# A state-space layer mixed with a feed-forward layer: own states for even tokens, B without scaling, and the skip as diagonal products

## Chip, core and metric

The kernel runs on one core of a Trainium2 chip. The metric is device time in microseconds (us) of one execution. Ratios are the mean time of one kernel's fast runs over the mean of the other's fast runs of the same rounds, so they are not quite the ratio of the medians that are quoted beside them. The profile's *span* runs from the first to the last instruction; the time is 1.7 to 2.1 us longer than the span.

Engines: PE (TensorE, matrix products), PEld (its weight loads, which overlap PE), DVE (VectorE), ACT (ScalarE), POOL (GpSimd), SP (SyncE, which issues most DMAs). PE's matmuls are pipelined: the mean length of one is not its cost, the distance to the next start is (448 columns: 0.35 us mean length, 0.19 us from start to start).

## The reference, cut to what matters

```python
# x: [1, 2048, 448] bf16; B, C: complex 448 x 448; Lambda, Dskip: 448; w1: 448 x 1792; w2: 1792 x 448
g = sigmoid((x * gate_w).sum(-1))
Lam_bar = exp(exp(log_dt) * Lam);  B_bar = ((Lam_bar - 1) / Lam)[:, None] * B
h[t] = Lam_bar * h[t-1] + B_bar @ x[t]                   # complex, 2048 steps
a = 2 * real(h @ C.T) + x * Dskip
b = silu(x @ w1) @ w2
out = g * a + (1 - g) * b
```

Both kernels take tokens in pairs: row k holds tokens 2k (even) and 2k+1 (odd). The 448 complex states lie in seven tiles of 128 rows: three pairs (real, imaginary) and one tile with 64 real and 64 imaginary rows. The recurrence over 1024 pairs is a scan on VectorE, turned into a real one by cos/sin tables.

## The kernel before

It builds `Lambda*B` on VectorE, so one product gives the input of a whole pair, and it scans only the odd tokens' states. The even token's output comes from the odd state before it, through a second matrix `CE` (C times Lambda), and from its own x through a dense matrix `K0 = C B + diag(Dskip)`:

```python
def bu(m, h):                       # input of a pair of tokens: 7 products of full height
    for j in range(7):
        pe.matmul(ps[bank], LT[:, m, j, :], XT[:, j, h*512:(h+1)*512], start=(j == 0), stop=(j == 6))
# ... (cut)
def k0(j):                          # K0, block j of 4
    for m in range(7):
        pe.matmul(ps[0:M, bank, 0:D], BB[:, m, D+j*128:D+j*128+M], CO[:, m, :], ...)
    pe.matmul(ps[0:M, bank, j*128:j*128+M], ID[:, 0:M], DE[:, j, 0:M], ...)        # + diag(Dskip)
# ... (cut)
def ytile(kt, odd):                 # output of 128 tokens
    for m in range(7):
        pe.matmul(ps[:, bank, 0:D], HS[:, m, o0:o0+128], C[:, m, :], ...)          # C = CO if odd else CE
    if not odd:
        for j in range(4):
            pe.matmul(ps[:, bank, 0:D], XT[:, j, t0:t0+128], KT[:, j, :], ...)     # x @ K0
    # DVE: out = gate * ps + BG (odd; BG = gate*x*Dskip + b, two DVE operations) or + b (even)
# ... (cut) the order near the end of PE's program
ffn2(3, 0); ffn2(3, 1)
for j in range(4): k0(j)
ffn2(3, 2); ffn2(3, 3)
for q in range(4): ytile(q, 0); ytile(q, 1); skip(q + 4); store(q)
for kt in range(4, 8): ytile(kt, 0); ytile(kt, 1); store(kt)
```

Of the kernel before, what the change touches and what calls it, by code (L numbers as in the profile page):

```python
# [146 lines left out]
def gated_mix(nc, A_x, A_Lambda_re, A_Lambda_im, A_B_re, A_B_im, A_C_re, A_C_im, A_log_dt,  # L147
              A_Dskip, B_x, B_w1, B_w2, gate_w, out):
    with ExitStack() as ctx:
# [9 lines left out]
        XT = sb("XT", [128, 7, NK], BF16)  # L159
        W1E = sb("W1E", [128, 4, F_FF], BF16)  # L160
        W1O = sb("W1O", [128, 4, F_FF], BF16)
        W2 = sb("W2", [128, NFB, D], BF16)
        BB = sb("BB", [128, 7, 2 * D], BF16)
        Y3 = sb("Y3", [128, 2, D], BF16)
        LT = sb("LT", [128, 8, 7, 128], BF16)
# [3 lines left out]
        CE = sb("CE", [128, 8, D], BF16)  # L169
        KT = sb("KT", [128, 4, D], BF16)  # L170
        DE = sb("DE", [128, 4, 128], BF16)
        DBC = sb("DBC", [128, D], BF16)
# [3 lines left out]
        HS = sb("HS", [128, 8, NK + 8], BF16)  # L176
        AT = [sb(f"AT{i}", [128, NFB, 512], BF16) for i in range(2)]
        OT = [sb(f"OT{i}", [128, 2 * D], BF16) for i in range(3)]
        GWB = sb("GWB", [128, D], BF16)
        JK = sb("JK", [128, 2, D], BF16)  # L180
# [4 lines left out]
        TMPS = [sb(f"TMP{i}", [128, D], F32) for i in range(2)]  # L185
# [9 lines left out]
        W1EF = W1E[:, :, :].rearrange("p a b -> p (a b)")  # L195
        XO = W1EF[:, 0:NKT * D].rearrange("p (k c) -> p k c", k=NKT)
        BG = W1EF[:, NKT * D:].bitcast(F32).rearrange("p (k c) -> p k c", k=4)
        LTF = LT[:, :, :, :].rearrange("p a b c -> p (a b c)")

        def bs(tile):  # L200
            return LTF[:, tile * D:(tile + 1) * D]

# [7 lines left out]
        def ldt(dst, src, key, reads=(), group=None):  # L210
            return T.dma("sp", lambda e: e.dma_start_transpose(dst, src), reads=reads,
                         writes=[key], group=group)

        XE = [[f"XTe0{j}" for j in range(4)], ["XTe1"] * 4]

        def swap_xr(eng, h):
            hs = slice(h * 512, (h + 1) * 512)
            T.op(eng, lambda e: e.tensor_copy(XR[64:128, hs], XT[0:64, 3, hs]), reads=XE[h][3:],
                 writes=[f"XR{h}a"])
            T.op(eng, lambda e: e.tensor_copy(XR[0:64, hs], XT[64:128, 3, hs]), reads=XE[h][3:],  # L220
                 writes=[f"XR{h}b"])
# [28 lines left out]
        T.op("act", lambda e: e.activation(JK[:, 0, 0:1], HP[:, :], AF.Exp), reads=["HP"], writes=["JK0"])  # L250
        ld("act", W1E[64:128, 3, :], B_w1[384:448, :], "W1Ez")
        ld("sp", BB[:, 0:6:2, D:], A_B_re[0:384, :].rearrange("(t p) d -> p t d", p=128), "Bre", gB)
        ld("sp", BB[:, 1:6:2, D:], A_B_im[0:384, :].rearrange("(t p) d -> p t d", p=128), "Bim", gB)
        ldt(XT[:, 0:4, 512:1024], x2[512:1024, 0:512], "XTe1")
        gB3 = T.group()
        for i, src in enumerate((A_B_re, A_B_im)):
            for h in range(2):
                ld("sp", Y3[h * 64:(h + 1) * 64, i, :], src[384:448, :], f"By{i}{h}", gB3)
        for h in range(2):
            ldt(XT[:, 4:7, h * 512:(h + 1) * 512], x2[h * 512:(h + 1) * 512, 512:896], f"XTo{h}")  # L260
        B_RAW = ["Bre", "Bim"]
        XC_ALL = ["XC0", "XC1"] + [f"XC3_{q}" for q in range(4)]
        B3 = ["By00", "By01", "By10", "By11"]

# [8 lines left out]
        T.op("pool", lambda e: e.memset(KT[64:128, 3, :], 0.0), writes=["KTz"])  # L273
        swap_xr("pool", 1)
# [10 lines left out]
        def ffn1_mm(c, fbs):  # L285
# [3 lines left out]
            W, w0, x0, jr = (W1O, 1, 4, 0) if odd else (W1E, 0, 0, 3)  # L289
            banks = [nxt() for _ in fbs]  # L290
            xk = XE[h] + [f"XTo{h}"] if odd else XE[h]

            for fb, bank in zip(fbs, banks):
                def mm(pe, fb=fb, bank=bank):
                    ins = None
                    for j in range(3):
                        ins = pe.matmul(ps[:, bank, :], W[:, w0 + j, fb * 128:(fb + 1) * 128],  # L297
                                        XT[:, x0 + j, hs], start=(j == 0), stop=False)
                    return ins
                wk = ["W1Ob"] if odd else ["W1Ej0", "W1Ej1", "W1Ej2"] if fb < NFA else ["W1Ed"]  # L300
                T.op("pe", mm, reads=wk + xk, writes=[f"ps{bank}"])

            def rest(pe):
                ins = None
                for i, (fb, bank) in enumerate(zip(fbs, banks)):
                    up = (i % 2 == 1) != bool(odd)
                    p = slice(64, 128) if up else slice(0, 64)
                    x = XT[p, 3, hs] if up == bool(odd) else XR[p, hs]
                    ins = pe.matmul(ps[:, bank, :], W[p, jr, fb * 128:(fb + 1) * 128], x,  # L309
                                    start=False, stop=True)  # L310
                return ins
            wk = ["W1Oa", "W1Oz"] if odd else ["W1Ea", "W1Ez"]
            T.op("pe", rest, reads=wk + xk + [f"XR{h}a", f"XR{h}b"],
                 writes=[f"ps{bank}" for bank in banks])
# [18 lines left out]
        def ffn1_act(c, fb, bank):  # L333
            a = AT[c % 2]
            T.op("act", lambda e: e.activation(a[:, fb, :], ps[:, bank, :], AF.Silu),  # L335
                 reads=[f"ps{bank}"], writes=[f"AT{c % 2}_{fb}"])

        def ffn1(c, f0=0):
            for f in range(f0, NFB, 4):
                for fb, bank in ffn1_mm(c, list(range(f, min(f + 4, NFB)))):  # L340
                    ffn1_act(c, fb, bank)
                    yield fb
# [32 lines left out]
        T.op("dve", lambda e: e.tensor_copy(XR[0:64, 0:512], xp[3][64:128, :]), reads=["ps6"], writes=["XR0b"])  # L375
# [36 lines left out]
        pact("dt", LDT, AF.Exp, ["PV"])  # L412
        ptt("ar", col("dt"), LRE, ALU.mult, ["dt", "PV"])
        pact("mag", col("ar"), AF.Exp, ["ar"])
        T.op("act", lambda e: e.activation(JK[:, 0, 0:1], HP[:, :], AF.Silu), reads=["HP"], writes=["JK0"])
        ptt("ph", col("dt"), LIM, ALU.mult, ["dt", "PV"])
# [3 lines left out]
        pts("nfr", col("fr"), -1.0, None, ALU.mult, ALU.bypass, ["fr"])  # L420
        ptt("afr", col("fr"), col("nfr"), ALU.max, ["fr", "nfr"])
        pact("sn", col("fr"), AF.Sin, ["fr"], scale=SIN_SCALE)
        pact("cs", col("afr"), AF.Sin, ["afr", "HP"], scale=-SIN_SCALE, bias=HP[:, 0:1])
        ptt("t0", LRE, LRE, ALU.mult, ["PV"])
        ptt("t1", LIM, LIM, ALU.mult, ["PV"])
        ptt("t0", col("t0"), col("t1"), ALU.add, ["t0", "t1"])
        T.op("dve", lambda e: e.reciprocal(col("rden"), col("t0")), reads=["t0"], writes=["rden"])
        ptt("lr", col("mag"), col("cs"), ALU.mult, ["mag", "cs"])
        ptt("li", col("mag"), col("sn"), ALU.mult, ["mag", "sn"])
        pts("nli", col("li"), -1.0, None, ALU.mult, ALU.bypass, ["li"])  # L430
        for o, up, low in (("ba", "lr", "li"), ("bb", "nli", "lr")):
            for a, b, n in ((0, 64, up), (64, 128, low)):
                T.op("dve", lambda e, o=o, a=a, b=b, n=n: e.tensor_copy(
                    P[a:b, pc(o), 3:4], P[a:b, pc(n), 3:4]), reads=[n], writes=[o])
        pc("dr")

# [5 lines left out]
            reads=["f2"] + SGN, writes=["f2s"])  # L442
        ptt("rr", col("mag"), col("mag"), ALU.mult, ["mag"])


        def phase(pt):
            return HS[:, 2 * pt:2 * pt + 2, :].rearrange("p a b -> p (a b)")[:, 0:2 * NK].bitcast(F32)

        def phases(pt):
            f2 = "f2s" if pt == 3 else "f2"  # L450
            X, RR = phase(pt), G[:, 1, :]
            T.op("dve", lambda e: e.tensor_scalar(X, IOTA[:, :], c1(f2, pt), None, ALU.mult),
                 reads=["IOTA", f2], writes=[f"F{pt}"])
            T.op("dve", lambda e: e.tensor_scalar(RR, X, MAGIC, -MAGIC, ALU.add, ALU.add),
                 reads=[f"F{pt}"], writes=["G1"])
            T.op("dve", lambda e: e.tensor_tensor(X, X, RR, ALU.subtract),
                 reads=[f"F{pt}", "G1"], writes=[f"F{pt}"])

        def tables(pt):
            X = phase(pt)  # L460
            T.op("act", lambda e: e.activation(SIN[:, pt, :], X, AF.Sin, scale=SIN_SCALE),
# [7 lines left out]
            T.op("pool", lambda e: e.memset(HS[:, 2 * pt:2 * pt + 2, 0:8], 0.0),  # L469
                 writes=[f"F{pt}", f"HSz{pt}"])  # L470
# [3 lines left out]
        n_tmp = [0]  # L474

        def lincombs(items):

            ts = []
            for dst, key, x, xs, y, ys, reads in items:
                t = n_tmp[0] % 2  # L480
                n_tmp[0] += 1
                ts.append(t)
                T.op("dve", lambda e, t=t, y=y, ys=ys: e.tensor_scalar(TMPS[t][:, :], y, ys, None, ALU.mult),
                     reads=reads, writes=[f"TMP{t}"])
            for (dst, key, x, xs, y, ys, reads), t in zip(items, ts):
                T.op("dve", lambda e, t=t, dst=dst, x=x, xs=xs: e.scalar_tensor_tensor(
                    dst, x, xs, TMPS[t][:, :], ALU.mult, ALU.add),
                    reads=list(reads) + [f"TMP{t}"], writes=[key])

        def step_B(pt):  # L490
            if pt < 3:
                lincombs([(BB[:, m, 0:D], f"BB{m}", BB[:, m, D:], c1("lr", pt), BB[:, m ^ 1, D:],
# [288 lines left out]
        for fb in ffn1(1):  # L781
            if fb % 3 == 1:
                run(tabs, 1)
# [91 lines left out]
```

## Time and profile before

| | |
|---|---|
| time, median of 3 runs | 154.72 us (154.54 to 158.25) |
| span of the profiled execution | 154.1 us |
| PE / DVE / ACT busy | 96% / 78% / 41% |

First the page of the kernel before: busy times of each engine, and its chain of waits by engine. The chain is followed back from the last instruction, at each step to what released it.

```profile
PE 148.0 (96%) x749; PEld 67.6 (44%) x749; DVE 120.2 (78%) x233; ACT 63.8 (41%) x111; POOL 5.5 (4%) x15
...
PE 91%; DMA 5%; SPq 1%; DVE 0%; issue 0%
```

The same chain in order of time (start, length, what):

```profile
2.46 8.44 DMA W1E<-in_B_w_dram
...
10.94 3.30 PE ps L324 x14
14.24 2.70 PE ps L297 x12
...
31.48 21.26 PE ps L643 x98
...
112.66 1.32 PE ps L658 x7
113.98 0.06 PE ps L660
...
123.67 1.32 PE ps L738 x7
125.00 0.76 PE ps L742 x4
125.75 2.65 PE ps L738 x14
...
150.95 0.68 DVE OT L750
```

From 10.94 us on, each piece starts where the last ended: the time is the sum of PE's work. L297 (with the half-height L309) belongs to the first feed-forward product, L627 to the second (FFN2), L658 and L660 are K0, L738 the state products of the output, L742 the even tiles' `x @ K0`, L643 the products by B.

Groups of instructions of the kernel before (line, engine, operation, shapes, count; then busy us, mean ns of one; then idle before):

```profile
L676 DVE TENSOR_TENSOR Q<-G,COS 128x1024 bf16<-128x1024 f32 x7 | 8.5, 1211 | 0.0
L676 DVE TENSOR_TENSOR Q<-HS,COS 128x1024 bf16<-128x1024 bf16 x7 | 4.8, 685 | 0.0
L486 DVE SCALAR_TENSOR_TENSOR CO<-XC,P,TMP 128x448 bf16<-128x448 bf16 x7 | 4.5, 673 | 0.0
```

These are VectorE's prices: 0.69 us for a 1024-wide product of two bf16 tiles, 1.21 us with a float32 input, and 0.67 us for a 448-wide scalar_tensor_tensor. What the prediction below calls "one element a cycle" is about 1.04 ns per element.

### The profile page before, as it was taken

How to read it: one execution, taken by the hardware profiler on the slowest of the kernel's cores; microseconds unless marked ns; L12 is line 12 of the kernel's file. 1: busy time of each engine (PE TensorE's matmuls, PEld its weight loads, DVE VectorE, ACT ScalarE, POOL GpSimd, SP SyncE). 2: the span in 40 equal slices, each digit the busy share in tenths (PEclk: the TensorE clock that was granted, in tenths of full speed). 3: DMA queues.
4: the chain of work that ended last, by engine and by line, in shares of the span. 5: the costliest groups of instructions: out<-in, count | busy, mean ns of one | idle time of the engine just before them, and what ended most of it. 6: DMA issues, size and time to landing. Idle time of an engine off the chain costs nothing.

```text
span 154.1 us, 1999 instructions
## 1 busy us (share of the span) xinstructions
PE 148.0 (96%) x749; PEld 67.6 (44%) x749; DVE 120.2 (78%) x233; ACT 63.8 (41%) x111; POOL 5.5 (4%) x15
## 2 busy tenths in 40 slices
PE   6879999999999999999999999999999999999991
PEld 2323333344444455433455333555555555555550
DVE  1653913999999999999999999999999218885341
ACT  1256748999976600555731166612233110000000
POOL 7000040000000000000000000000000000000000
PEclk9999999999999999999999999999999999999999
DMA  4999999998942930004834500000000001112211
GB/s 125 279 234 226 221 355 164 219 175 147 345 124 55 304 117 0 0 22 93 156 85 96 187 0 4 0 2 0 0 0 4 0 0 60 60 60 83 100 60 60
DMA packets 26225, 16.25 MB, mean 105 GB/s; under 512 B 17892, under 2 KB 25320, under 8 KB 26216
## 3 DMA queue, kind: packets, MB, share of 16 engines
q1 hardware_dynamic: 24452, 13.23, 35.2%
q10 hardware_dynamic: 1764, 2.90, 7.2%
q8 instruction: 6, 0.10, 0.3%
q14 instruction: 3, 0.02, 0.0%
HBM read 9.93 MB, written 1.84 MB: 76 GB/s over the span
## 4 chain that ended last, share of the span: by engine, by line
PE 91%; DMA 5%; SPq 1%; DVE 0%; issue 0%
PE ps L627 28%; PE ps L297 21%; PE ps L643 14%; PE ps L738 14%; DMA W1E<-in_B_w_dram 5%; PE ps L309 4%; PE ps L742 4%; PE ps L658 4%; PE ps L324 2%; SPq L208 1%; DVE OT L750 0%; SPq L237 0%; PE ps L660 0%
## 5 line engine op out<-in xcount | busy, mean ns | idle before, releaser
L627 PE MATMUL ps<-W,AT 128*128 128x448 bf16 x224 | 43.1, 353 | 0.0
L335 ACT ACTIVATE AT<-ps 128x512 bf16<-128x512 f32 x56 | 29.0, 606 | 13.9 <-PE ps L309 11.9
L627 PEld LDWEIGHTS ps<-W,AT 128*128 128x128 bf16 x224 | 21.7, 98 | 20.6 <-ACT AT L335 0.5
L632 ACT ACTIVATE LT<-ps,GT 128x448 bf16<-128x448 f32 x16 | 9.8, 634 | 32.8 <-PE ps L627 23.2
L643 PE MATMUL ps<-XT,LT 128*128 128x512 bf16 x98 | 21.3, 379 | 0.0
L297 PE MATMUL ps<-XT,W1O 128*128 128x512 bf16 x84 | 19.5, 380 | 0.0
L679 DVE TENSOR_TENSOR_SCAN G<-P,Q 128x1024 f32<-128x1024 f32 x7 | 15.7, 2277 | 0.0
L297 PE MATMUL ps<-XT,W1E 128*128 128x512 bf16 x63 | 14.6, 380 | 0.0
L643 PEld LDWEIGHTS ps<-XT,LT 128*128 128x128 bf16 x98 | 9.5, 98 | 11.5 <-issue 0.2
L750 DVE SCALAR_TENSOR_TENSOR OT<-ps,GT,LT 128x448 bf16<-128x448 f32 x8 | 5.5, 684 | 9.7 <-PE ps L742 9.6
L297 PEld LDWEIGHTS ps<-XT,W1O 128*128 128x128 bf16 x84 | 7.7, 98 | 10.9 <-issue 2.5
L738 PE MATMUL ps<-CE,HS 128*128 128x448 bf16 x56 | 11.9, 352 | 0.0
L738 PE MATMUL ps<-CO,HS 128*128 128x448 bf16 x56 | 11.9, 352 | 0.0
L750 DVE SCALAR_TENSOR_TENSOR OT<-ps,GT,W1E 128x448 bf16<-128x448 f32 x8 | 5.5, 684 | 5.1 <-PE ps L738 5.1
L297 PEld LDWEIGHTS ps<-XT,W1E 128*128 128x128 bf16 x63 | 5.7, 98 | 8.6 <-issue 1.7
L647 ACT ACTIVATE HS<-ps 128x512 bf16<-128x512 f32 x14 | 8.0, 609 | 2.6 <-PE ps L643 2.0
L594 DVE SCALAR_TENSOR_TENSOR JK<-W1O,GWB 128x448 bf16<-128x448 bf16 x16 | 8.8, 621 | 0.0
L676 DVE TENSOR_TENSOR Q<-G,SIN 128x1024 bf16<-128x1024 f32 x7 | 8.5, 1220 | 0.0
L676 DVE TENSOR_TENSOR Q<-G,COS 128x1024 bf16<-128x1024 f32 x7 | 8.5, 1211 | 0.0
L324 PE MATMUL ps<-XT,W1E 128*128 128x512 bf16 (+1 forms) x28 | 6.8, 379 | 1.3 <-DMA W1E<-in_B_w_dram 1.0
L738 PEld LDWEIGHTS ps<-CE,HS 128*128 128x128 bf16 x56 | 5.5, 98 | 5.1
L738 PEld LDWEIGHTS ps<-CO,HS 128*128 128x128 bf16 x56 | 5.5, 98 | 5.1
(84 smaller groups left out, 147.5 us busy)
## 6 DMA issues: line engine op xcount, KB each, us to landing
W1O<-in_A_x_dram ACTq DMA_DIRECT2D x1, 1792.0 KB, 11.6
out_dram<-OT SPq DMA_DIRECT2D x8, 224.0 KB, 1.9
W<-in_B_w_dram SPq DMA_DIRECT2D x1, 1568.0 KB, 7.7
W1O<-in_B_w_dram SPq DMA_DIRECT2D x1, 1344.0 KB, 8.4
W1E<-in_A_x_dram SPq DMA_DIRECT2D x1, 896.0 KB, 6.2
W1E<-in_B_w_dram ACTq DMA_DIRECT2D x3, 224.0 KB, 7.4
W1E<-in_B_w_dram SPq DMA_DIRECT2D x1, 672.0 KB, 10.4
W1E<-in_B_w_dram SPq DMA_DIRECT2D x2, 224.0 KB, 6.3
```

Of the source, the lines that this page charges most:

```text
L297: ins = pe.matmul(ps[:, bank, :], W[:, w0 + j, fb * 128:(fb + 1) * 128], XT[:, x0 + j, hs], start=(j == 0), stop=False)
L324: T.op("pe", lambda pe, fb=fb, bank=bank, j=j, p=p: pe.matmul(ps[:, bank, :], W1E[p, j, fb * 128:(fb + 1) * 128], XT[p, j, 0:512], start=( ...
L335: T.op("act", lambda e: e.activation(a[:, fb, :], ps[:, bank, :], AF.Silu), reads=[f"ps{bank}"], writes=[f"AT{c % 2}_{fb}"])
L594: T.op("dve", lambda e, t=t: e.scalar_tensor_tensor(JK[:, t % 2, :], XN[:, t * D:(t + 1) * D], 1.0, GWB[:, :], ALU.mult, ALU.mult, accum_o ...
L627: ins = pe.matmul(ps[:, bank, 0:D], a[:, fb, q * 128:(q + 1) * 128], W2[:, fb, :], start=(fb == 0), stop=(fb == NFB - 1))
L632: T.op("act", lambda e: e.activation(bs(tile), ps[:, bank, 0:D], AF.Copy, scale=GT[:, 2, tile:tile + 1]), reads=[f"ps{bank}", "GT2"], writ ...
L643: ins = pe.matmul(ps[:, bank, :], LT[:, m, j, :], XT[:, j, h * 512:(h + 1) * 512], start=(j == 0), stop=(j == 6))
L647: T.op("act", lambda e: e.activation(HS[:, m, 8 + h * 512:8 + (h + 1) * 512], ps[:, bank, :], AF.Copy), reads=[f"ps{bank}", f"F{pt}"], wri ...
L676: T.op("dve", lambda e: e.tensor_tensor(o, a, b, op), reads=reads, writes=writes)
L679: T.op("dve", lambda e: e.tensor_tensor_scan(G[:, c, :], rb, Q1[:, c, :], 0.0, ALU.mult, ALU.add), reads=[f"Q1{c}", "rr"], writes=[f"G{c}"])
L738: ins = pe.matmul(ps[:, bank, 0:D], HS[:, m, o0:o0 + 128], C[:, m, :], start=(m == 0), stop=(odd == 1 and m == 6))
L750: T.op("dve", lambda e: e.scalar_tensor_tensor(o[:, odd * D:(odd + 1) * D], ps[:, bank, 0:D], GT[:, 1, tile:tile + 1], BG[:, kt % 4, :] if ...
```

## The change

The intent: take the dense K0 off PE. Even tokens get states of their own: B is used as it is (DMA transposes bring it and odd x into place), PE gives the inputs of even and odd tokens apart, and VectorE combines them before the scan and makes the even states after it. Both kinds of tile then need only the matrix CO. The skip becomes four diagonal products in each output tile. The gate sums go to ScalarE, the phases partly to POOL, and all queues get a new order; PE opens eight odd tiles before the last state pair is ready.

```diff
-        def bu(m, h):   # 7 full-height products with Lambda*B | B
+        def bu(pt, h):  # even and odd apart: 3 full-height products each ...
+            for odd, banks in ((0, be), (1, bo)):
+                for m, bank in zip(ms, banks):
+                        for j in range(3):
+                            ins = pe.matmul(ps[:, bank, :], bt(slice(0, 128), j, m), XT[:, 4 * odd + j, hs], ...)
+            def rest(pe):   # ... and one of half height (64 rows) each
+                    for odd, bank in ((0, b0), (1, b1)):
+                        p = slice(64 * odd, 64 * odd + 64)
+                        ins = pe.matmul(ps[:, bank, :], bt(p, 3, m), XT[p, 4 * odd + 3, hs], ...)
...
-        def k0(j): ...
+            # in scan(pt), before: input of the pair = Lambda * even input + odd input
+                stt(G[:, :, w], ve[:, :, w], lr, u[:, :, w], ...)
+                stt(u[:, 0, w], ve[:, 1, w], nli, G[:, 0, w], ...)
+                stt(u[:, 1, w], ve[:, 0, w], li, G[:, 1, w], ...)
+            # after: even state = Lambda * odd state before + even input
+            stt(G[:, :, :], hp, lr, ve, ...)
+            stt(ve[:, 0, :], hp[:, 1, :], nli, G[:, 0, :], ...)
+            stt(ve[:, 1, :], hp[:, 0, :], li, G[:, 1, :], ...)
...
-        def ytile(kt, odd): ...
+        YA, YB = (0, 1, 6, 2, 3), (4, 5)
+        def yopen(kt, odd):
+                for m in YA:
+                    ins = pe.matmul(ps[:, bank, 0:D], state(kt, odd, m), CO[:, m, :], start=(m == 0), stop=False)
+                for j in range(3):      # the skip: a diagonal block of 128 columns each
+                    ins = pe.matmul(ps[:, bank, j * 128:(j + 1) * 128], XT[:, 4 * odd + j, xr], DE[:, j, :], ...)
+                return pe.matmul(ps[:, bank, 384:D], XT[p, 4 * odd + 3, xr], DE[p, 3, p], ...)   # 64 rows
+        def yclose(kt, odd, bank): ...  # the two products of YB, then DVE: out = gate * ps + b
...
+        opened = [(kt, 1, yopen(kt, 1)) for kt in range(8)]
+        for o in opened:
+            yclose(*o)
+        for kt in range(8):
+            yclose(kt, 0, yopen(kt, 0))
```

## The prediction

> **What bounds it now.** The chain of waits is 91% TensorE (PE) and, apart from 8.4 us of W1E load, has no gap: matmuls run from 10.9 us to 150.9 us of the 154.1 us span; then one eviction (0.68 us) and the last store. VectorE (DVE) is busy 120 us (78%) and close to full from 27 to 120 us, but nothing on the chain waits for it until the last tile. ScalarE (ACT) is at 41%. So the time is the sum of PE's work.
>
> **Removed from PE** (chain durations): the K0 product 5.6 us, and the even tiles' product of x with K0, 8 x 0.76 = 6.1 us.
> **Added:** the skip as four diagonal products in each of 16 tiles. Short 128-column products cost 60 to 78 ns each in the trace (the 16 start transposes took 1.25 us), so about 0.3 us per tile, 4.8 us. The projection by B becomes 84 whole and 28 half-height products; half ones cost 135 ns each in the feed-forward, so 21.9 us instead of 21.3. Net: PE does about 6.2 us less. With no new gap the span would be near 147.7 us.
>
> **Moved.** DVE loses about 18 us of B/C/CE scaling, 10 us of skips, half of the gates (16 x 0.62 + reads, to 4 x 1.09) and half of the phases. It gains, for each of three state pairs, about 9.7 us: two blocks of one 2048-wide and two 1024-wide scalar_tensor_tensor. These run at one element a cycle here (448 wide: 0.67 us), so I estimate 2.33 and 1.27 us. The Trainium skill ("VectorE: DVE Perf Modes", perf-mode tier table) gives tensor_tensor 2x for bf16 and 1x for fp32; the trace agrees (1024 wide: 0.69 and 1.22 us). A pair costs about 24 us in all, the half pair 13. Total DVE is again about 120 us.
>
> From the first scan to the last state, DVE has about 99 us in one order. It can start once transposed x has landed, at 27 to 31 us, and waits 1 to 3 us for the gate's copy of x. The last states are then ready at 128 to 132 us. PE opens eight odd tiles without the last pair, so it should need the odd states of that pair at about 132 us: little or no wait, but little slack.
>
> ACT gains 16 gate sums (about 0.65 us), the doubled B evictions and the C scaling, to 80-85 us. Its bad place is 34 to 57 us: 16 sums, a sine table and five activations stand in one queue with PSUM evictions, so PE should lose about 3 us to banks in the first half-projection of FFN2 and the next B products.
>
> DMA: B's and odd x's transposes come before XN. I estimate 0 to 3 us of PE wait before the first B product at 20 us.
>
> **Prediction:** 147.7 + 1 + 3 = 152 us of span by this sum; the bank wait is perhaps overestimated, so I say 151.2 us, 80% range 147.5 to 155. Chances: faster by over 2% 0.55, within 2% 0.41, slower 0.04.
>
> **What would show it.** PE busy 6 us less with the K0 lines gone; wait rows for PE on ACT between 40 and 62 us (about 3 us) and on transposes near 20 us (about 1); DVE over 90% busy from 30 to 130 us; the chain still mostly PE; scalar_tensor_tensor 2048 near 2.33 us; diagonal products at 75 ns.
>
> **What would make it wrong.** Broadcast cos/sin dropping tensor_tensor to 1x (+1.07 us for each of 12), so that DVE ends at 140+ and even tiles wait; transposes slower than thought, delaying scans; POOL phases slow; or ACT's gate sums not holding PE at all (then 148).

## The result, and the profile after

Median 152.31 us (151.98 to 152.56, 4 runs) against 154.86 us; ratio 0.9836, 95% interval 0.9816 to 0.9856. All four runs of the changed kernel are fast; one of before's four, 158.25 us, is slow and is left out of the ratio. The kernel became 1.6% faster.

The page of the changed kernel:

```profile
PE 144.0 (96%) x756; PEld 64.7 (43%) x763; DVE 119.6 (80%) x148; ACT 81.8 (54%) x130; POOL 15.1 (10%) x20
...
PE 80%; ACT 12%; DMA 3%; DVE 2%; issue 1%
```

Its chain of waits in order of time:

```profile
18.19 0.92 ACT AT L333
...
19.25 2.84 PE ps L625 x12
22.08 0.54 PE ps L635 x4
...
45.52 0.92 ACT AT L333
...
46.48 5.47 PE ps L597 x28
...
119.51 0.95 PE ps L754 x5
120.45 0.17 PE ps L756 x3
120.62 0.13 PE ps L758
...
147.23 0.68 DVE OT L781
```

L625 and L635 are the products by B, of full and half height; L754 and L774 the state products of the output; L756 the three diagonal products of 128 columns, L758 the fourth, of 64 rows and 64 columns. The chain goes over ACT where PE waited for a bank, a slice of PSUM that ACT had still to empty. How long PE waited is in the waits of PE:

```profile
PE ps L625 <- ACT AT L333: 0.7, 1, 0.7
PE ps L297 <- issue: 0.4, 2, 0.3
PE ps L597 <- ACT AT L333: 0.3, 1, 0.3
```

The middle row is almost no wait. At both of its places the trace has twelve weight loads and only eleven matmuls: the record of the first matmul (about 0.22 us) is missing. At the second place the first weight load starts at 24.35 us, where the products by B ended at 24.34 us.

VectorE's prices and its place after (groups, then the last rows of its timeline before the output stage):

```profile
L655 DVE SCALAR_TENSOR_TENSOR G<-HS,P,VE 128x2048 f32<-128x2048 bf16 x3 | 7.0, 2350 | 0.1
L571 ACT ACTIVATE XN<-XN 128x448 bf16<-128x448 bf16 x16 | 9.0, 564 | 0.0
```

```profile
123.05 2.48 DVE L655 SCALAR_TENSOR_TENSOR VE<-HS,P,G 128x1024 bf16<-128x1024 bf16 x2
130.74 5.71 DVE L781 SCALAR_TENSOR_TENSOR OT<-ps,GT,XN 128x448 bf16<-128x448 f32 x9 [5.21 <-PE ps L774]
```

VectorE had its last state at 125.5 us and then stood idle for 5.2 us until PE closed the first odd tile.

POOL's share of the phases had a side effect. The Trainium skill ("GPSIMD Engine Reference", Specifications) says that POOL shares its SBUF interfaces with VectorE, which contend when VectorE has two SBUF inputs. The trace agrees: tiny VectorE operations of this kind ended when POOL's did, and took 1.0 us where the same kind takes 0.16 us; and a POOL operation beside a 1024-wide VectorE one took 2.08 us where its like took 1.16 us (spans on POOL are rough). VectorE's rows, then POOL's, of the timeline of after:

```profile
12.26 1.23 DVE L451 SCALAR_TENSOR_TENSOR FP<-G,FP 128x1024 f32<-128x1024 f32 x1 [1.08 <-POOL G L446]
...
17.96 1.01 DVE L479 TENSOR_TENSOR P<-P,SG 128x1 f32<-128x1 f32 x1
```

```profile
9.93 1.16 POOL L444 TENSOR_SCALAR FP<-IOTA,P 128x1024 f32<-128x1024 f32 x1 [5.73 <-DVE P L409]
...
12.39 2.08 POOL L444 TENSOR_SCALAR Q<-IOTA,P 128x1024 f32<-128x1024 f32 x1 [0.17 <-POOL G L446]
...
17.93 1.04 POOL L446 TENSOR_SCALAR G<-FP 128x1024 f32<-128x1024 f32 x1
```

Read stage by stage from the two chains: K0 is gone (-5.6 us). The output stage did **not** shrink: 123.67 to 150.95 us is 27.3 us before, 119.51 to 147.23 us is 27.7 us after. The products by B went from 21.3 us to 22.7 us. PE waits about 1.0 us for banks, in the first and third row above. The feed-forward products behind half-height products by B take 2.70 us for twelve where they took 2.59 us, twice: 0.2 us. The sum, -5.6 + 0.4 + 1.4 + 1.0 + 0.2 = -2.6 us, is close to the -2.5 us of the times.

The profile of before has a trap. It shows a span of 154.1 us, but the seven runs of before in the first set of experiments had spans of 152.7 to 154.3 us, median 153.0 us, and after's four runs 149.9 to 150.5 us, median 150.2 us. The difference between the two shown profiles, 4.0 us, is therefore about 1.2 us too large (see e5_before_again).

### The profile page after: what moved, and what is told of

It reads as the page before. It is cut to its first block, busy times and chain, and to the rows that moved or that the text cites. A ratio compares the mean times of both kernels' runs of the same rounds, so it can differ in the third digit from the quotient of the medians.

```text
span 150.1 us, 1958 instructions
## 1 busy us (share of the span) xinstructions
PE 144.0 (96%) x756; PEld 64.7 (43%) x763; DVE 119.6 (80%) x148; ACT 81.8 (54%) x130; POOL 15.1 (10%) x20
## 4 chain that ended last, share of the span: by engine, by line
PE 80%; ACT 12%; DMA 3%; DVE 2%; issue 1%
PE ps L597 25%; PE ps L297 16%; PE ps L625 13%; PE ps L754 11%; ACT AT L333 5%; PE ps L774 5%; PE ps L309 3%; ACT XN L571 3%; PE ps L635 3%; DMA CO<-in_A_x_dram 3%; PE ps L756 2%; ACT COS L461 2%; PE ps L758 1%; ACT SIN L456 1%; PE ps L322 1%; DVE P L409 1%
## 5 line engine op out<-in xcount | busy, mean ns | idle before, releaser
L297 PE MATMUL ps<-XT,W1E 128*128 128x512 bf16 x142 | 33.5, 380 | 0.6 <-issue 0.4
L333 ACT ACTIVATE AT<-ps 128x1024 bf16<-128x1024 f32 (+1 forms) x32 | 27.2, 918 | 6.5 <-PE ps L309 6.5
L781 DVE SCALAR_TENSOR_TENSOR OT<-ps,GT,XN 128x448 bf16<-128x448 f32 x16 | 10.4, 680 | 12.0 <-PE ps L774 11.9
L602 ACT ACTIVATE XN<-ps,GT 128x448 bf16<-128x448 f32 x16 | 9.6, 630 | 16.3 <-PE ps L597 16.3
L625 PE MATMUL ps<-XT,BT 128*128 128x512 bf16 x70 | 16.2, 380 | 0.8 <-ACT AT L333 0.7
L625 PEld LDWEIGHTS ps<-XT,BT 128*128 128x128 bf16 x72 | 6.6, 97 | 10.1 <-issue 2.4
L571 ACT ACTIVATE XN<-XN 128x448 bf16<-128x448 bf16 x16 | 9.0, 564 | 0.0
L754 PE MATMUL ps<-CO,HS 128*128 128x448 bf16 x40 | 8.9, 354 | 0.0
L754 PE MATMUL ps<-CO,VE 128*128 128x448 bf16 x40 | 8.9, 353 | 0.0
L655 DVE SCALAR_TENSOR_TENSOR HS<-VE,P,G 128x512 bf16<-128x512 bf16 (+1 forms) x8 | 7.8, 1015 | 0.1
L309 PE MATMUL ps<-XT,W1E 64*128 64x512 bf16 x25 | 7.8, 382 | 0.0
L309 PE MATMUL ps<-XR,W1E 64*128 64x512 bf16 x24 | 7.6, 382 | 0.0
```

The lines of the kernel that those rows point to most:

```text
L297: ins = pe.matmul(ps[:, bank, :], W1E[:, j, fb * 128:(fb + 1) * 128], XT[:, x0 + j, hs], start=(j == 0), stop=False)
L309: ins = pe.matmul(ps[:, bank, :], W1E[p, 3, fb * 128:(fb + 1) * 128], x, start=False, stop=True)
L333: T.op("act", lambda e: e.activation(a[:, fb:fb + n, :], ps[:, bank:bank + n, :], AF.Silu), reads=[f"ps{bank + i}" for i in range(n)], wri ...
L571: T.op("act", lambda e, t=t, v=v: e.activation(v, v, AF.Copy, accum_out=Z[:, t:t + 1]), reads=[f"XG{t // 4}"], writes=[f"Z{t}", f"BS{t}"])
L602: T.op("act", lambda e: e.activation(bs(tile), ps[:, bank, 0:D], AF.Copy, scale=GT[:, 2, tile:tile + 1]), reads=[f"ps{bank}", "GT2"], writ ...
L625: ins = pe.matmul(ps[:, bank, :], bt(slice(0, 128), j, m), XT[:, 4 * odd + j, hs], start=(j == 0), stop=False)
```

## The experiments

Each ratio is to the kernel before, run in the same rounds. Theory: the time is the sum of PE's work and its waits, VectorE is off the path, and the gain of K0 was partly spent on products of half height. Rivals: VectorE's order of states limits; short products in a row cannot hide their weight loads; ScalarE's gate sums hold PE.

### e1_before_no_k0: K0 alone

```diff
-        T.op("pool", lambda e: e.memset(KT[64:128, 3, :], 0.0), writes=["KTz"])
+        T.op("pool", lambda e: e.memset(KT[:, :, :], 0.0), writes=["KTz"])
...
-        for j in range(4):
-            k0(j)
```

> The kernel before with the K0 product left out (its result filled with zeros; the output is wrong on purpose). Theory 'the time is the sum of TensorE's work': the 5.6 us of K0 on the chain go, so 149.2 us, ratio to before 0.964, and all other stages keep their lengths. Rival 'VectorE is the hidden limit before the output stage': it finishes C at 115.3 us and the last skip at 120.3 us, so the output stage would start later than 118.1 us or show waits on VectorE, and less than 4 us would be gained.

Its output is wrong, which doesn't matter for the time. Measured: 149.04 us against 154.69 us, ratio 0.9635 (0.9579 to 0.9691). The 5.65 us are K0's 5.6 us on the chain. VectorE was no hidden limit in the kernel before.

### e2_after_no_skip: what the diagonal products cost

```diff
-                for j in range(3):
-                    ins = pe.matmul(... XT[:, 4 * odd + j, xr], DE[:, j, :], ...)
-                return pe.matmul(ps[:, bank, 384:D], XT[p, 4 * odd + 3, xr], DE[p, 3, p], ...)
+                return ins
```

> The changed kernel without the diagonal products (output wrong on purpose). By the record's cost of 0.30 us a tile it should gain 4.8 us on the changed kernel (ratio to before about 0.953). If, as the output stage's length after suggests (27.7 us against 21.2 us for 112 products of 0.19 us), a tile's skip costs 0.41 us, it gains 6.5 us (ratio about 0.942). If VectorE, which ends its states at 125.5 us, is the limit, it gains under 4 us and TensorE waits for it.

Its output is wrong, which doesn't matter for the time. Measured: 145.85 us, ratio 0.9415 (0.9365 to 0.9464). That is 6.5 us under the changed kernel's 152.31 us: 0.40 us for each of 16 tiles, not the 0.30 us on record. The sparse skip of all tiles cost PE as much as the dense `x @ K0` of the even ones (8 x 0.76 = 6.1 us); the odd tiles' skip was on VectorE before.

### e3_skip_full_height and e4_skip_mixed: why so much

In e3 the fourth diagonal product reads all 128 rows; the added rows of the diagonal are zero in those columns. In e4 the diagonal products also stand one by one between long products.

```diff
 # e3
-   return pe.matmul(ps[:, bank, 384:D], XT[p, 4 * odd + 3, xr], DE[p, 3, p], start=False, stop=False)
+   return pe.matmul(ps[:, bank, 384:D], XT[:, 4 * odd + 3, xr], DE[:, 3, p], start=False, stop=False)
 # e4, besides
+   for j, m in enumerate(YA):
+       ins = pe.matmul(... state(kt, odd, m), CO[:, m, :], ...)
+       if j < 3:    pe.matmul(... XT[:, 4 * odd + j, xr], DE[:, j, :], ...)
+       elif j == 3: pe.matmul(ps[:, bank, 384:D], XT[:, 4 * odd + 3, xr], DE[:, 3, p], ...)
```

> The changed kernel, with the fourth diagonal product of each tile over all 128 rows (the other half of the diagonal block's column range is zero) in place of 64. If the switch between half-height and full-height products costs time, a tile loses about 0.1 us, so 1.6 us in all (ratio to before about 0.973). If the cost lies in short products in a row, whose weight loads cannot hide, nothing changes (0.984).

> As e3, and the four diagonal products stand one by one between the long state products. If the excess of the skip over its 187 ns of columns (0.22 us a tile) is weight loads that have no long product to hide behind, the whole of it goes: 3.5 us less than the changed kernel (ratio to before about 0.961). If each short product costs the same wherever it stands, it equals e3.

Measured: e3 149.04 us, ratio 0.9625 (0.9579 to 0.9671), correct; e4 149.08 us, ratio 0.9625 (0.9575 to 0.9675), correct. One even tile in the chain of after, then one in the chain of e3:

```profile
133.35 0.95 PE ps L754 x5
134.30 0.17 PE ps L756 x3
134.46 0.13 PE ps L758
134.60 0.48 PE ps L774 x2
```

```profile
131.82 0.94 PE ps L754 x5
132.76 0.17 PE ps L756 x3
132.93 0.03 PE ps L758
132.96 0.38 PE ps L774 x2
```

The product of half height cost 0.10 us more for itself and 0.10 us more for the product behind it: 0.2 us a tile, 3.3 us in all, twice what e3's expectation allowed for (the cost comes at entering and at leaving). The product now reads twice the rows and is still cheaper. Three full-height diagonal products in a row need 0.17 us, which at 57 ns each is close to their 54 ns of columns, an estimate from 448 columns in 0.189 us (1.32 us for seven); the theory of weight loads without cover falls, as e4's equal time says too. The Trainium skill has the mechanism ("TensorEngine Tiling (Array Packing)", Key Properties): "Changing tiling mode (not just tile) drains the TensorE". It gives no figure; here a change cost about 0.1 us each way. The runs show this price of a change of height; that a drain is its reason is the page's word, which no run tests.

### e5_before_again: is the profile of before typical?

No edit: the kernel before, profiled once more.

> The kernel before, unchanged, profiled again. Its shown profile has a span of 154.1 us, while the other runs of it that were timed have spans of 152.7 to 153.4 us, and it waited for the first weights until 10.9 us. If that wait belongs to this one execution, a second profile shows a span near 153.0 us, the first feed-forward group done near 12.9 us instead of 14.2 us, and every later stage of equal length. If the change really brings the weights sooner, this profile again shows 14.2 us.

Measured: 154.08 us, one run of unknown state, with a span of 152.3 us (153.0 us was expected). Its chain:

```profile
7.74 4.74 PE ps L324 x21
12.48 2.70 PE ps L297 x12
...
149.20 0.68 DVE OT L750
```

Compare 14.24 us for the second line in the profile first shown. The wait for weights until 10.9 us belonged to that one execution; it is no gain of the change, and later stages are equal (the output stage is again 27.3 us, K0 5.6 us).

### e6_table_later and e10_early_order: the waits before 25 us

```diff
 # both, on top of e3
-        run(t0)                 # first cos/sin table on ACT
         run(ffn1(0, NFA))
+        run(t0)
 # e10 besides
-        phases2(2)
         swap_xr("dve", 1, 0)
+        phases2(2)
```

> As e3 (the diagonal product at full height, 149.0 us), with the first cos/sin table behind the activations of the first feed-forward stage in ScalarE's order, not before. If TensorE's wait of 0.6 to 0.7 us ahead of the first B product is for banks held behind that table, this gains 0.6 us: 148.4 us, ratio to before about 0.959. If something else would end that wait just as late (the transposes of B and x), nothing is gained: 0.9625.

> As e6 (table later), and the swap of x's half block that the next feed-forward group needs stands one instruction earlier on VectorE, ahead of the phases of the third pair. In e6 TensorE's wait did not go away: it came back as 0.9 us in front of that group, which reads the swapped block, ready at 24.38 us. If the wait is for this swap, 0.6 to 0.9 us go: about 148.2 us, ratio to before 0.957. If x's transposes land no sooner, or the bank wait near 46 us grows by as much, the time stays at 149.0 us (0.962).

Measured: e6 148.98 us, ratio 0.9618 (0.9593 to 0.9642); e10 148.32 us, ratio 0.9581 (0.9556 to 0.9606); both correct. In e6 the bank wait vanished, and PE waited elsewhere; its timeline of PE:

```profile
18.54 2.76 PE L625 MATMUL ps<-XT,BT 128*128 128x512 bf16 x12
...
24.48 2.75 PE L297 MATMUL ps<-XT,W1E 128*128 128x512 bf16 x12 [0.92 <-issue]
```

The profile says "issue", for it found no releaser. The product reads a block that VectorE's copy had ready at 24.38 us; e10 moved that copy forward (ready at 23.76 us), and the wait fell to about 0.15 us: its profile says 0.37 us, but again one matmul record of 0.22 us is missing. So a wait removed came back at the next dependence, and two edits gained together what the first alone could not; the second alone was not run. e10 is 0.7 us under e3. The intervals of the two ratios touch, but the spans do not: 145.9 to 146.5 us against 146.7 to 147.1 us. (The two ran on different chips, where before's medians were 154.79 and 154.69 us.)

### e7_scan_twice and e8_scan_thrice: VectorE's slack

```diff
 # on top of e3, in scan(pt)
-            sc(0, pt)
-            sc(1, pt)
+            for _ in range(2 if pt == 2 else 1):      # 3 in e8
+                sc(0, pt)
+                sc(1, pt)
```

> As e3, with the two scans of the last state pair done twice: 4.5 us more VectorE work before the last states. If TensorE's work sets the time and VectorE has slack there, at most 0.2 us is lost (ratio to before 0.9625 to 0.964). If VectorE's order of states is the limit, 4.5 us are lost (about 0.992).

> As e7 with the two scans done three times: 9.0 us more VectorE work. The states would then end at 135.6 us by e3's profile, where even tiles start at 131.7 us and need one odd eviction (0.7 us) first, so 4.5 us are lost against e3 (ratio to before about 0.992). If VectorE were the limit already, 9 us are lost (about 1.02); if it had far more slack, nothing.

Measured: e7 148.47 us, ratio 0.9581 (0.9547 to 0.9616), no loss for 4.4 us more work on VectorE. (It is even 0.6 us under e3, for a cause that was not found: 0.3 us of it lies outside the span. So small differences between programs need care.) e8 152.14 us, ratio 0.982 (0.9772 to 0.9869), which is unclear by the 2% rule: 3.1 us over e3, where 4.5 us were expected and 9 if VectorE were the limit. Its two runs at full clock have spans of 149.5 us, 2.6 us over e3's. VectorE has over 4 us of slack and is not the limit; the rival falls. In e8's profile PE waits 2.30 us for an eviction, and soon after runs slowly; at 138.4 us the granted clock, which is 1.00 at full speed, is 1.00 again. Stretches of e8: us, busy time of each engine with counts, granted clock (PEclk), DMA share, GB/s.

```profile
131.80:134.10 2.30, 0.02 (x1) 0.03 (x2) 2.30 (x4) 0.00 (x0) 0.00 (x0) 1.00 0.00 0
134.10:136.30 2.20, 2.20 (x12) 1.16 (x13) 2.12 (x4) 0.00 (x0) 0.00 (x0) 0.68 0.40 139
136.30:138.40 2.10, 2.10 (x10) 0.97 (x9) 2.08 (x5) 0.00 (x0) 0.00 (x0) 0.52 0.53 181
```

Finer windows put the fall between 134.6 and 135.2 us: 1.00 before, 0.50 from 135.2 to 137.7 us. Two of e8's four runs had a mean clock of 1.0 and were 1.5 us shorter (151.34 and 151.48 us against 152.79 and 153.01 us at 0.989, the profiled one among them). So this wait may have cost more than its length, but that is not shown: whether the two shorter runs waited as long is not on record, and e9's three slow runs below have the same mean clock (0.987 to 0.989).

### e9_gate_on_dve and e12_gate_on_dve_2: the gate sums

```diff
 # on top of e3
-   T.op("dve", ... e.tensor_tensor(v, v, GWB..., ALU.mult), ...)                   # 4 times
-   T.op("act", ... e.activation(v, v, AF.Copy, accum_out=Z[:, t:t + 1]), ...)      # 16 times
+   T.op("dve", ... e.scalar_tensor_tensor(v, v, 1.0, GWB[:, :], ALU.mult, ALU.mult,
+                                          accum_out=Z[:, t:t + 1]), ...)           # 16 times
 # e12: the tanh keeps its place in ACT's order
```

> As e3 (149.0 us, ratio to before 0.9625), but the 16 gate sums go back to VectorE (multiply and sum in one instruction, as before), so ScalarE's queue of 34 to 57 us loses its 16 sums. The prediction on record put 3 us of bank wait on that queue: by it this gains up to 3 us. The trace of after shows one such wait of 0.26 us in the second half of FFN2's first tiles, so at most 0.3 us can be gained; and VectorE gets about 6 us more, of which by e7 and e8 about 5 us are free, so the time is from 0.3 us shorter to 1.5 us longer (0.960 to 0.972).

> The e9 experiment again with its flaw mended: in e9 the tanh of all gates had moved up in ScalarE's order and held the activations behind it until VectorE had all sums (a wait of 1.8 us). Here the tanh keeps its place after the last activation of this stage, and only the 16 sums leave ScalarE. If ScalarE's sums held TensorE by 3 us, as the prediction on record had it, this beats e3 (149.0 us, ratio 0.9625) by 2 to 3 us. By the trace of after (one wait of 0.26 us) it gains at most 0.3 us; VectorE's 6 us more end its states at about 131.7 us in place of 126.6, where even tiles start, so it may lose up to 1 us: ratio 0.960 to 0.969.

e9 measured a median of 151.51 us (149.38 to 153.29); three of six runs were slow, and by its fast runs the ratio is 0.967 (0.9636 to 0.9704). It is inconclusive: the tanh had slipped forward in ACT's order and held PE for 1.8 us, a flaw of the experiment. e12: 147.88 us, ratio 0.9575 (0.9541 to 0.961), correct. Its profile has no wait of PE near 46 us; from the start of FFN2's first tiles to the next products by B it took 10.6 us instead of e3's 11.0 us. So the sums held PE by about 0.4 us there, not 3 us. The rest of e12's 1.2 us against e3 was not pinned down: 0.3 us of it lies outside the span, and the products before 41 us also ran 0.4 us earlier in that run.

### e13_all_three

The edits of e10 and e12 together.

> The three edits that won, together: full-height last diagonal product, first table and half-block swap in e10's order, gate sums on VectorE. If e10's 0.7 us (waits ahead of the first B product and the next feed-forward group) and e12's gain (bank wait near 46 us) are separate waits of TensorE, they add: about 147.2 us, ratio to before about 0.952. If VectorE, whose states end within 1 us of the first odd eviction in e12, has become the limit, nothing is gained over e12 (0.9575).

Measured: 148.10 us, ratio 0.9569 (0.954 to 0.9597), correct. Nothing is added to e12. In the profiled run PE waited 0.8 us in the middle of the first product by B, before the products with odd x, a wait that e10's run did not have. PE's own row says "issue"; the row of its weight loads, idle for 1.27 us up to the same place, names the DMA transpose of x. Such releasers are inferred, and no run isolates this one. e10, e12 and e13 all beat both given kernels; between the three no difference is shown.

## Why the prediction was right, and where its sum was not

The measured 152.31 us lies in the range (147.5 to 155), 1.1 us above the 151.2 us; the class was "within 2%", to which 0.41 was given, while "faster by over 2%", held likelier at 0.55, did not come. The sum, 152 us, was of span, where after has 150.2 us; 151.2 us is compared with a time, so the gap of about 2 us between the two was passed over. The mechanism, PE's work as the limit and VectorE off the path, was right. That the number came so near is partly luck, for the sum came out by errors that cancelled:

| term | on record | shown | by |
|---|---|---|---|
| K0 removed | -5.6 us | -5.6 us | e1 |
| even `x @ K0` removed | -6.1 us | -6.1 us | chain of before |
| diagonal skip added | +4.8 us | +6.5 us | e2; 3.3 us of it is the change of height, e3 |
| B products | +0.65 us | +1.4 us | chains; same pattern as e3, no run isolates it |
| feed-forward products behind half-height B products | none | +0.2 us | chains |
| wait for transposes | +1 us | none in after's profile | waits of after |
| bank waits on ACT | +3 us | +0.7 us behind a table, +0.3 us behind the sums | waits of after, e6, e12 |
| waits put down to "issue" | none | almost none: 0.4 us in the view, where two matmul records are missing | PE and its weight loads in after |

- **Mis-sized: the skip.** The price was taken from short products that stood among their like (60 to 78 ns). The fourth product of each tile, with 64 rows between products of 128, was priced as if its height cost nothing. At full height all four take 0.20 us (e3), less than the 0.30 us on record; the change of height adds 0.2 us. Without it "faster" would have come (e3: 0.9625). The half-height products by B were priced from a row of four (0.54 us, so 135 ns each). A row of two takes 0.32 us, so that mean holds the change on entering, but not the one on leaving: in e3's chain twelve full products by B take 2.59 us behind full ones and 2.70 us behind half-height ones.
- **Mis-sized: the ACT wait.** The wait behind the gate sums was put at about 3 us and was 0.3 to 0.4 us (after, e12). One gate sum was put at 0.65 us; it took 0.56 us from start to start. The skill's formula for an ACTIVATE with immediate operands ("ScalarE: Activation LUTs", What ACT_TABLE_LOAD costs: 186 ns + 0.833 ns per element) gives an estimate of 0.559 us for 448, and the trace has 0.564 us; the 0.19 us read of each sum overlaps its neighbours. Using it would have made the sixteen sums 1.4 us shorter (16 x 0.09), about half of the 2.7 us by which the wait was overestimated; why so little of the queue reached PE was not tested. The wait ahead of the first B product, behind the cos/sin table, was not foreseen at its place.
- **The starting point.** 154.1 us of span was a long execution of before; the typical 153.0 us would have lowered the sum by 1.1 us, to 150.9 us of span (measured 150.2 us).
- **VectorE was right.** Estimates of 2.33 and 1.27 us for the new operations, trace 2.35 and 1.28 us; cos/sin spread over two tiles kept the bf16 price (2048 wide: 1.22 us, 1024 wide: 0.69 us); states ready at 125.5 us where 128 to 132 us were expected; no wait of PE on them.
- **Open.** Before's time is 1.7 us over its span, after's 2.1 us (e7, e8, e9 and e12 1.8 us). The span shows -2.8 us where the time shows -2.5 us. What lies outside the span was not found.

## What to carry to other kernels

Here a product of half height among full ones cost about 0.1 us more at each end; where zero rows are at hand, try the full-height product, which took 0.03 us in place of 0.13 us. Price an operation from a place in the trace with the same neighbours, not from one among its like. Before a prediction, compare the shown span with the spans of the timed runs, and after removing a wait look for the next dependence, since the wait may just move there. Before believing a short wait of PE, compare its matmuls with its weight loads: a missing record looks like a wait.

## What the Trainium skill lacked or had wrong

- "TensorEngine Tiling (Array Packing)", Key Properties, says that a mode change drains PE but not the price: about 0.1 us on entering and 0.1 us on leaving a 64-row product (0.13 against 0.03 us, and 0.48 against 0.38 us, e3).
- "TensorE: Matmul & The Clock Gate", Why this matters for your kernels, warns of idle gaps over about 3 us. In e8's profile a shorter gap, 2.30 us, was followed within about 1 us by a granted clock of 0.50. One profile shows it; that the gap was the cause is not shown.
